# A gated GELU layer on one core: the first slices of x by plain loads in token halves on two queues, all transposed by TensorE

## The chip, the core and the metric

The kernel runs on one NeuronCore of a Trainium2 chip. A core has TensorE (matrix products; PE in the profile, its weight loads PEld), VectorE (DVE), ScalarE (ACT), GpSimd (POOL) and SyncE (SP). SP and ACT also issue the DMAs that bring data from device memory into the core's memory; an issue is shown under SPq or ACTq. The metric is the device time of one execution in microseconds, the median of several runs.

## What is computed

```python
def _gelu(x):
    return jax.nn.gelu(x, approximate=True)

# x: 1 x 2048 x 1024, w_gate and w_up: 1024 x 3584, w_down: 3584 x 1024, all bfloat16
def reference(x, w_gate, w_up, w_down):
    g = jnp.einsum("bsd,df->bsf", x, w_gate)
    u = jnp.einsum("bsd,df->bsf", x, w_up)
    h = _gelu(g) * u
    return jnp.einsum("bsf,fd->bsd", h, w_down)
```

## The kernel before

The 2048 tokens are worked in two halves of 1024, each half in two chunks of 512 (`c`). For one half the kernel first computes h transposed (`hT`: 28 blocks of 128 hidden features by 1024 tokens), then the product with w_down (`down`, line 306) and stores it.

The 28 blocks come in eight groups (`GROUPS`, 3 or 4 blocks). For each block and chunk there are two sums in two PSUM banks, gate and up, of eight matmuls each: over `ko`, the eight slices of 128 of the model dimension (`mm1`, line 103; the stationary operand is a 128x128 piece of weight, the moving one a 128x512 slice of x transposed, `xT[c][ko]`). `Evac` takes a pair of banks through ScalarE and VectorE to hT. Weights go through rings of three (`wg`, `wu`), filled group by group from SP by `wload`; `wd`, the seven 1 MB pieces of w_down, is loaded from SP between the groups of the first half.

x must stand with the model dimension on the partitions. Everywhere but in the opening this is done by DMA transposes from SP (`xload`, line 98). In the opening, chunk 0 of the first half comes in two ways: slices 0 to 5 by plain loads into `xn` (line 186, two slices and all 512 tokens in one DMA of 256 KB) and four 128x128 TensorE transposes each (`turn`, line 230), copied from PSUM to `xT` by VectorE (lines 236, 239, 240; slice 0 in two halves from two banks); slices 6 and 7 by two DMA transposes from SP, after the plain loads. `NTURN` is the number of slices that TensorE turns.

The order of the instructions of each engine is the order in which the program writes them (`manual_schedule`). TensorE begins with six dummy matmuls on a constant (line 174), `turn(0)`, two more dummies of 512 and 256 columns, and then `first_group`: for each slice `ko` the six matmuls of group 0 (three blocks, gate and up), with the turn of slice `ko + 1` set between them. In slice 0 the three gate matmuls go first, then the turn, then the three up matmuls. ScalarE's queue has the load of the activation table (line 180), one small Square on a zeroed tile (`gate`, `gated`, lines 178 and 181), and then its share of the opening's DMAs; SP has the rest. Weights of group 0 are loaded slice by slice (line 192; 96 KB for one slice, 192 KB for two). After the opening's loads SP issues the weights of groups 1 and 2 (line 89), then the eight DMA transposes of chunk 1.

DMAs tell of their landing on eight semaphores in turn, so the ninth issue waits for the first landing, the tenth for the second, and so on.

Group 1 begins with `ahead=2` (gate sums of two blocks, then their up sums) while group 0 is evacuated.

Of the kernel before, what the change touches and what calls it, by code (L numbers as in the profile page):

```python
# [14 lines left out]
def kernel(  # L15
# [11 lines left out]
    nc = tc.nc  # L27
    P = nc.NUM_PARTITIONS
    bf16 = mybir.dt.bfloat16
    f32 = mybir.dt.float32  # L30
    ACT = mybir.ActivationFunctionType
    ALU = mybir.AluOpType

    x2 = x.flatten_outer_dims()
    out2 = out.flatten_outer_dims()
    S, Dm = x2.shape
    Df = w_gate.shape[1]
    NKB = Dm // P
    NFB = Df // P
    SCH = 512  # L40
# [11 lines left out]
    NTMP = 3  # L52
    NST = 4
    WDF = 4
    NWARM = 6
    NTURN = 6
    TPC = SCH // P

    pool = ctx.enter_context(tc.tile_pool(name="sb", bufs=1))
    psum = ctx.enter_context(tc.tile_pool(name="ps", bufs=1, space=bass.MemoryType.PSUM))  # L60

    xT = [[pool.tile([P, SCH], bf16, name=f"xT{c}_{k}") for k in range(NKB)] for c in range(HSC)]
    hT = [pool.tile([P, HS], bf16, name=f"hT{f}") for f in range(NFB)]
    wd = [pool.tile([P, WDF, Dm], bf16, name=f"wd{i}") for i in range(NFB // WDF)]
# [8 lines left out]
    ident = pool.tile([P, P], bf16, name="ident")  # L73
    xn = [pool.tile([P, TPC, 2 * P], bf16, name=f"xn{q}") for q in range(NTURN // 2)]
    banks = [psum.tile([P, 512], f32, name=f"bank{b}") for b in range(8)]
# [3 lines left out]
    def bank():  # L79
        nonlocal nbank  # L80
        b = banks[nbank % 8]
        nbank += 1
        return b
# [12 lines left out]
    def xload(half, c, ko):  # L96
        s0 = half * HS + c * SCH
        nc.sync.dma_start_transpose(
            out=xT[c][ko], in_=x2[s0 : s0 + SCH, ko * P : (ko + 1) * P]
        )  # L100

    def mm1(ps, w, j, c, ko):
        nc.tensor.matmul(  # L103
            ps,
            lhsT=w[:, ko, j * P : (j + 1) * P],
            rhs=xT[c][ko],
            start=(ko == 0),
            stop=(ko == NKB - 1),
        )

# [38 lines left out]
    def pair(wg, wu, j, f, c):  # L149
        g_ps, u_ps = bank(), bank()  # L150
        for ko in range(NKB):
            mm1(g_ps, wg, j, c, ko)
        for ko in range(NKB):
            mm1(u_ps, wu, j, c, ko)
        evac(g_ps, u_ps, f, c)
# [11 lines left out]

    ctx.enter_context(tc.manual_schedule())

    gate = pool.tile([P, SCH], bf16, name="gate")  # L170
    gated = pool.tile([P, 1], f32, name="gated")

    def dummy(b, n=SCH):
        nc.tensor.matmul(b[:, :n], lhsT=warm[:, :P], rhs=warm[:, :n], start=True, stop=True)  # L174

    nc.vector.memset(gate, 0.0)  # L178
    make_identity(nc, ident)
    nc.scalar.preload_act_table(ACT.Sigmoid)  # L180
    nc.scalar.activation(gated, gate[:, :1], ACT.Square)
    for _ in range(NWARM):
        dummy(banks[5])

    def xpart(eng, ko, n):
        eng.dma_start(
            out=xn[ko // 2][:, :, (ko % 2) * P : (ko % 2 + n) * P],
            in_=x2[0:SCH, ko * P : (ko + n) * P].rearrange("(t p) d -> p t d", p=P),
        )

    def wpart(eng, ring, w, ko, n):
        eng.dma_start(
            out=ring[0][:, ko : ko + n, : GROUPS[0] * P],
            in_=w[ko * P : (ko + n) * P, : GROUPS[0] * P].rearrange("(ko ki) f -> ki ko f", ki=P),
        )


    S, A = nc.sync, nc.scalar
    G, U = (wg_ring, w_gate), (wu_ring, w_up)
    xpart(S, 0, 2)  # L200
    wpart(A, *G, 0, 1)
    wpart(S, *U, 0, 1)
    wpart(A, *G, 1, 1)
    wpart(A, *U, 1, 1)
    xpart(S, 2, 2)
    xpart(A, 4, 2)
    wpart(S, *G, 2, 1)
    wpart(S, *U, 2, 1)
    wpart(S, *G, 3, 1)
    wpart(A, *U, 3, 1)  # L210
    wpart(S, *G, 4, 2)
    wpart(A, *U, 4, 2)
    wpart(S, *G, 6, 2)
    wpart(A, *U, 6, 2)
    for ko in range(NTURN, NKB):
        xload(0, 0, ko)
    for n in (1, 2):
        wload(nc.sync, wg_ring, w_gate, n, n)
        wload(nc.sync, wu_ring, w_up, n, n)
# [3 lines left out]
    def turn(ko):  # L223


        tp = [banks[6 + ko % 2].bitcast(bf16)] * 2
        if ko == 0:
            tp = [banks[6].bitcast(bf16), banks[7].bitcast(bf16)]
        for t in range(TPC):
            nc.tensor.transpose(  # L230
                tp[t // (TPC // 2)][:, t * P : (t + 1) * P],
                xn[ko // 2][:, t, (ko % 2) * P : (ko % 2 + 1) * P],
                ident,
            )
        if ko:
            nc.vector.tensor_copy(out=xT[0][ko], in_=tp[0][:, :SCH])  # L236
        else:
            h = SCH // 2
            nc.vector.tensor_copy(out=xT[0][ko][:, :h], in_=tp[0][:, :h])  # L239
            nc.vector.tensor_copy(out=xT[0][ko][:, h:], in_=tp[1][:, h:SCH])  # L240
# [4 lines left out]
    def prefetch(n):  # L245
        if n < len(order):
            wload(nc.sync, wg_ring, w_gate, order[n][1], n)
            wload(nc.sync, wu_ring, w_up, order[n][1], n)

    def first_group():  # L250
        wg, wu = wg_ring[0], wu_ring[0]
        ps = [(bank(), bank()) for _ in range(GROUPS[0])]
        turn(0)
        dummy(banks[5])
        dummy(banks[5], SCH // 2)
        n0 = GROUPS[0]
        for ko in range(NKB):
            steps = [(b, j) for j in range(n0) for b in range(2)]
            if ko == 0:
                steps = [(b, j) for b in range(2) for j in range(n0)]  # L260
            for i, (b, j) in enumerate(steps):
                mm1(ps[j][b], (wg, wu)[b], j, 0, ko)
                if i == (2 if ko == 0 else 1) and ko + 1 < NTURN:
                    turn(ko + 1)
        e = [Evac(ps[j][0], ps[j][1], j, 0) for j in range(GROUPS[0])]
        e[0].square()
        e[1].square()
        e[0].cubic()
        e[0].sigmoid()
        e[1].cubic()  # L270
        e[2].square()
        e[0].gelu()
        e[0].product()
        e[1].sigmoid()
        e[2].cubic()
        e[1].gelu()
        e[1].product()
        e[2].sigmoid()
        e[2].gelu()
        e[2].product()  # L280

    def group(n, chunks, ahead=0):
        g = order[n][1]
        wg, wu = wg_ring[n % NW], wu_ring[n % NW]
        if ahead:
            pairs(wg, wu, range(ahead), STARTS[g], chunks[0])
        for j in range(ahead, GROUPS[g]):
            for c in chunks:
                pair(wg, wu, j, STARTS[g] + j, c)
# [13 lines left out]
    def down(half, ss, c0, cw, k):  # L303
        ps = bank()
        for f in range(NFB):
            nc.tensor.matmul(  # L306
                ps[:, :cw],
                lhsT=hT[f][:, ss * P : (ss + 1) * P],
                rhs=wd[f // WDF][:, f % WDF, c0 : c0 + cw],
                start=(f == 0),  # L310
                stop=(f == NFB - 1),
            )
        store(ps, half * HS + ss * P, c0, cw, k)

    for half in range(NHALF):
        base = half * NG
        if half == 0:
            first_group()
            group(1, [0], ahead=2)
            group(2, [0])  # L320
            for g in range(NG):
                group(g, [1] if g < NW else range(HSC))
                i = g - 1
                if 0 <= i < len(wd):
                    for q in range(i, len(wd) if g == NG - 1 else i + 1):
                        nc.sync.dma_start(
                            out=wd[q],
                            in_=w_down[q * WDF * P : (q + 1) * WDF * P, :].rearrange(
                                "(fo fi) d -> fi fo d", fi=P
                            ),  # L330
                        )
                prefetch(g + 3)
        else:
            for g in range(NG):
                group(base + g, range(HSC))
                prefetch(base + g + 3)
        k = 0
        xnext = [(c, ko) for c in range(HSC) for ko in range(NKB)] if half + 1 < NHALF else []
        for ss in range(HS // P):
            for dc in range(NDC):  # L340
                last = half == NHALF - 1 and ss == HS // P - 1 and dc == NDC - 1
                if last:
                    down(half, ss, dc * DMW, DMW // 2, 1)
                    down(half, ss, dc * DMW + DMW // 2, P, 1)
                    down(half, ss, dc * DMW + DMW - P, P, 0)
                else:
                    down(half, ss, dc * DMW, DMW, k)
                k += 1
                if xnext:
                    c, ko = xnext.pop(0)  # L350
                    xload(half + 1, c, ko)
# [30 lines left out]
```

## Time and profile before

| what | value |
| --- | --- |
| median of three runs | 591.14 us (590.63 to 591.17) |
| the profiled execution | 591.7 us, of which the span from its first instruction to its last 589.9 us |
| matmuls of gate and up in the trace (L103) | 1756, 426.4 us busy |
| matmuls of the down product (L306) | 935, 193.0 us busy |
| TensorE transposes (L230) | 24, 2.7 us busy |
| copies of turned slices, 128x512 (L236) | 5 of 425 ns |
| dummies (L174) | 8, 3.6 us busy |
| DMA transposes (L98) | 26 in all, of these 2 for chunk 0 |
| DMA traffic | 45.51 MB, mean 77 GB/s |

An execution is recorded instruction by instruction. Matmuls overlap in the pipeline, so a matmul's own duration (380 ns for 512 columns) is longer than the distance to the next, and the distance is what counts. A group's row names the line, engine, operation and tiles, the shape, the number, the busy time and mean, and the idle time ahead of it with what ended it. The chain of waits is followed back from the last instruction to what released each one; a stretch on the chain is time that nothing hid. A few matmul records are missing. Idle time of an engine that is off the chain costs nothing by itself.

### The profile page before, as it was taken

The page shows a single profiled execution, that of the slowest core. Times are in us where ns is not written, and L with a number is a line of the kernel's source. Part 1 is how long each engine was busy: PE and PEld are TensorE (multiplying, and loading weights), DVE is VectorE, ACT ScalarE, POOL GpSimd, SP SyncE. Part 2 cuts the span into 40 slices and gives each one's busy share as a digit, 9 for nine tenths or more (in the row PEclk, how much of TensorE's full clock was granted, in tenths as well). Part 3 has the DMA queues.
Part 4 walks back from the last instruction along what each step waited for, and adds up shares of the span by engine and source line. Part 5 has one row for each costly group of instructions (what it writes and reads, how often), then busy time and mean ns, then how long its engine had stood idle before and what let it go on. Part 6 is the DMA issues. An engine that isn't in the chain of part 4 may idle for free.

```text
span 589.9 us, 6587 instructions
## 1 busy us (share of the span) xinstructions
PE 583.4 (99%) x2723; PEld 269.0 (46%) x2776; DVE 244.2 (41%) x361; ACT 147.7 (25%) x243; POOL 0.7 (0%) x6
## 2 busy tenths in 40 slices
PE   9999999999999999999999999999999999999998
PEld 4444444444444444444444444444444444444445
DVE  1765665565656400000046565656556562000000
ACT  1433333333333200000023333333333331000000
POOL 0000000000000000000000000000000000000000
PEclk9999999999999999999999999999999999999999
DMA  8906936055050311111203034214000000000000
GB/s 233 222 10 186 316 104 214 13 202 178 1 178 1 107 48 42 45 46 36 54 19 108 17 126 143 86 57 131 12 1 1 1 2 9 19 27 19 27 19 27
DMA packets 57789, 45.51 MB, mean 77 GB/s; under 512 B 15776, under 2 KB 54176, under 8 KB 57760
## 3 DMA queue, kind: packets, MB, share of 16 engines
q1 hardware_dynamic: 56112, 44.05, 24.8%
q10 hardware_dynamic: 1648, 1.05, 0.6%
q8 instruction: 21, 0.34, 0.2%
q14 instruction: 8, 0.07, 0.0%
HBM read 37.49 MB, written 4.19 MB: 71 GB/s over the span
## 4 chain that ended last, share of the span: by engine, by line
PE 98%; DMA 1%; issue 0%; ACT 0%
PE bank L103 65%; PE bank L306 33%; DMA xn<-in_x_dram 1%; PE bank L230 0%; PE bank L174 0%; ACT st L298 0%
## 5 line engine op out<-in xcount | busy, mean ns | idle before, releaser
L103 PE MATMUL bank<-xT,wg 128*128 128x512 bf16 x880 | 213.8, 380 | 0.9
L103 PE MATMUL bank<-xT,wu 128*128 128x512 bf16 x876 | 212.6, 379 | 1.0
L306 PE MATMUL bank<-wd,hT 128*128 128x512 bf16 (+2 forms) x935 | 193.0, 366 | 0.9
L306 PEld LDWEIGHTS <-hT 128*128 128x128 bf16 x952 | 90.9, 98 | 102.9
L103 PEld LDWEIGHTS <-wg 128*128 128x128 bf16 x896 | 87.8, 98 | 105.6 <-issue 0.6
L103 PEld LDWEIGHTS <-wu 128*128 128x128 bf16 x896 | 87.7, 98 | 105.0
L125 ACT ACTIVATE sq<-bank 128x512 f32<-128x512 f32 x112 | 66.7, 596 | 172.7 <-PE bank L103 166.8
L136 DVE TENSOR_TENSOR tt<-sg,bank 128x512 bf16<-128x512 bf16 x112 | 77.0, 687 | 75.9 <-ACT sg L133 75.8
L128 DVE SCALAR_TENSOR_TENSOR wq<-sq,bank 128x512 f32<-128x512 f32 x112 | 76.9, 687 | 65.2 <-ACT sq L125 65.2
L133 ACT ACTIVATE sg<-wq 128x512 bf16<-128x512 f32 x112 | 70.5, 629 | 88.3 <-DVE wq L128 88.3
L300 DVE CAST st<-bank 128x512 bf16<-128x512 f32 (+2 forms) x17 | 11.1, 652 | 178.3 <-PE bank L306 166.9
L139 DVE TENSOR_TENSOR hT<-tt,bank 128x512 bf16<-128x512 bf16 x112 | 77.0, 687 | 12.4 <-DVE tt L136 0.9
L298 ACT CAST st<-bank 128x512 bf16<-128x512 f32 (+1 forms) x17 | 9.6, 566 | 178.1 <-PE bank L306 178.1
L236 DVE COPY xT<-bank 128x512 bf16<-128x512 bf16 x5 | 2.1, 425 | 6.2 <-PE bank L230 6.2
L174 PE MATMUL bank<-const-bfloat16-1.0 128*128 128x512 bf16 (+1 forms) x8 | 3.6, 601 | 0.8 <-PEq L366 0.8
L230 PEld LDWEIGHTS <-xn 128*128 128x128 bf16 x24 | 2.1, 111 | 2.7 <-DMA xn<-in_x_dram 1.2
L230 PE MATMUL bank<-ident,xn 128*128 128x128 bf16 x24 | 2.7, 247 | 0.3 <-DMA xn<-in_x_dram 0.3
L174 PEld LDWEIGHTS <-const-bfloat16-1.0 128*128 128x128 bf16 x8 | 1.0, 138 | 1.8 <-issue 1.8
L239 DVE COPY xT<-bank 128x256 bf16<-128x256 bf16 x1 | 0.3, 292 | 3.1 <-PE bank L230 3.1
L180 ACT ACT_TABLE_LOAD x1 | 1.3, 1283 | 0.7 <-PEq L366 0.7
L178 DVE MEMSET gate<- 128x256 uint32 x1 | 0.3, 272 | 0.9 <-PEq L366 0.9
masks.py:199 POOL TENSOR_SCALAR_AFFINE_SELECT ident<-ident 128x128 bf16<-128x128 bf16 x1 | 0.3, 292 | 0.1
(7 smaller groups left out, 1.1 us busy)
## 6 DMA issues: line engine op xcount, KB each, us to landing
wg<-in_w_gate_dram SPq DMA_DIRECT2D x8, 1024.0 KB, 5.4
wu<-in_w_up_dram SPq DMA_DIRECT2D x8, 1024.0 KB, 7.0
wd<-in_w_down_dram SPq DMA_DIRECT2D x7, 1024.0 KB, 8.8
wg<-in_w_gate_dram SPq DMA_DIRECT2D x7, 768.0 KB, 4.7
wu<-in_w_up_dram SPq DMA_DIRECT2D x7, 768.0 KB, 6.6
out_dram<-st SPq DMA_DIRECT2D x31, 128.0 KB, 1.7
xn<-in_x_dram SPq DMA_DIRECT2D x2, 256.0 KB, 4.0
xT<-in_x_dram SPq DMA_TRANSPOSE x26, 2.6
```

The source lines that it names most:

```text
L103: nc.tensor.matmul(ps, lhsT=w[:, ko, j * P : (j + 1) * P], rhs=xT[c][ko], start=(ko == 0), stop=(ko == NKB - 1),)
L125: nc.scalar.activation(self.sq, self.g, ACT.Square, scale=GELU_SQRT_C)
L128: nc.vector.scalar_tensor_tensor(out=self.wq, in0=self.sq, scalar=1.0, in1=self.g, op0=ALU.add, op1=ALU.mult)
L133: nc.scalar.activation(self.sg, self.wq, ACT.Sigmoid, scale=GELU_K)
L136: nc.vector.tensor_tensor(out=self.tt, in0=self.sg, in1=self.g, op=ALU.mult)
L139: nc.vector.tensor_tensor(out=self.dst, in0=self.tt, in1=self.u, op=ALU.mult)
L174: nc.tensor.matmul(b[:, :n], lhsT=warm[:, :P], rhs=warm[:, :n], start=True, stop=True)
L230: nc.tensor.transpose(tp[t // (TPC // 2)][:, t * P : (t + 1) * P], xn[ko // 2][:, t, (ko % 2) * P : (ko % 2 + 1) * P], ident,)
L236: nc.vector.tensor_copy(out=xT[0][ko], in_=tp[0][:, :SCH])
L298: nc.scalar.copy(out=st[:, :cw], in_=ps[:, :cw])
L300: nc.vector.tensor_copy(out=st[:, :cw], in_=ps[:, :cw])
L306: nc.tensor.matmul(ps[:, :cw], lhsT=hT[f][:, ss * P : (ss + 1) * P], rhs=wd[f // WDF][:, f % WDF, c0 : c0 + cw], start=(f == 0), stop=(f = ...
```

## The change

The two DMA transposes of chunk 0 go; all eight slices are loaded plainly and turned by TensorE (`NTURN` 8, `xn` one pair larger). Each pair of slices is loaded in two DMAs of 128 KB, tokens 0 to 255 from SP and tokens 256 to 511 from ACT. The order on the two queues is the same: a half of a pair of x, the weights of the two slices that use it (gate from SP, up from ACT), the next pair, and so on; the last two slices of weight come in one DMA each, as before.

The table load moves behind ACT's DMAs, and the zeroed tile with its memset and small Square is dropped. The number of dummies ahead of `turn(0)` stays six (`NWARM` 7, less one); the two after it become 256 and 128 columns in place of 512 and 256.

In slice 0 the three gate matmuls are split into six of 256 columns, first those of tokens 0 to 255 for the three blocks, then those of tokens 256 to 511; `turn(1)` still follows the last of them, ahead of the up matmuls. Only the first of a bank's matmuls carries the start flag.

The first three of the seven wd loads are issued in two halves of 512 KB each.

```diff
--- before.py
+++ after.py
@@ -52,8 +52,11 @@
     NTMP = 3
     NST = 4
     WDF = 4
-    NWARM = 6
-    NTURN = 6
+    NWARM = 7
+    NTURN = 8
+
+
+    NSPLIT = 3
     TPC = SCH // P
 
     pool = ctx.enter_context(tc.tile_pool(name="sb", bufs=1))
@@ -99,12 +102,13 @@
             out=xT[c][ko], in_=x2[s0 : s0 + SCH, ko * P : (ko + 1) * P]
         )
 
-    def mm1(ps, w, j, c, ko):
+    def mm1(ps, w, j, c, ko, t0=0, t1=SCH):
+
         nc.tensor.matmul(
-            ps,
+            ps[:, t0:t1],
             lhsT=w[:, ko, j * P : (j + 1) * P],
-            rhs=xT[c][ko],
-            start=(ko == 0),
+            rhs=xT[c][ko][:, t0:t1],
+            start=(ko == 0 and t0 == 0),
             stop=(ko == NKB - 1),
         )
 
@@ -167,25 +171,17 @@
 
     ctx.enter_context(tc.manual_schedule())
 
-    gate = pool.tile([P, SCH], bf16, name="gate")
-    gated = pool.tile([P, 1], f32, name="gated")
-
     def dummy(b, n=SCH):
         nc.tensor.matmul(b[:, :n], lhsT=warm[:, :P], rhs=warm[:, :n], start=True, stop=True)
 
-
-
-    nc.vector.memset(gate, 0.0)
     make_identity(nc, ident)
-    nc.scalar.preload_act_table(ACT.Sigmoid)
-    nc.scalar.activation(gated, gate[:, :1], ACT.Square)
-    for _ in range(NWARM):
+    for _ in range(NWARM - 1):
         dummy(banks[5])
 
-    def xpart(eng, ko, n):
+    def xpart(eng, ko, n, t0=0, t1=TPC):
         eng.dma_start(
-            out=xn[ko // 2][:, :, (ko % 2) * P : (ko % 2 + n) * P],
-            in_=x2[0:SCH, ko * P : (ko + n) * P].rearrange("(t p) d -> p t d", p=P),
+            out=xn[ko // 2][:, t0:t1, (ko % 2) * P : (ko % 2 + n) * P],
+            in_=x2[t0 * P : t1 * P, ko * P : (ko + n) * P].rearrange("(t p) d -> p t d", p=P),
         )
 
     def wpart(eng, ring, w, ko, n):
@@ -195,25 +191,31 @@
         )
 
 
+
+
     S, A = nc.sync, nc.scalar
     G, U = (wg_ring, w_gate), (wu_ring, w_up)
-    xpart(S, 0, 2)
-    wpart(A, *G, 0, 1)
-    wpart(S, *U, 0, 1)
-    wpart(A, *G, 1, 1)
-    wpart(A, *U, 1, 1)
-    xpart(S, 2, 2)
-    xpart(A, 4, 2)
-    wpart(S, *G, 2, 1)
-    wpart(S, *U, 2, 1)
-    wpart(S, *G, 3, 1)
-    wpart(A, *U, 3, 1)
-    wpart(S, *G, 4, 2)
-    wpart(A, *U, 4, 2)
+
+    def xhalves(ko, n):
+        xpart(S, ko, n, 0, TPC // 2)
+        xpart(A, ko, n, TPC // 2, TPC)
+
+    xhalves(0, 2)
+    for ko in (0, 1):
+        wpart(S, *G, ko, 1)
+        wpart(A, *U, ko, 1)
+    xhalves(2, 2)
+    for ko in (2, 3):
+        wpart(S, *G, ko, 1)
+        wpart(A, *U, ko, 1)
+    xhalves(4, 2)
+    for ko in (4, 5):
+        wpart(S, *G, ko, 1)
+        wpart(A, *U, ko, 1)
+    xhalves(6, 2)
     wpart(S, *G, 6, 2)
     wpart(A, *U, 6, 2)
-    for ko in range(NTURN, NKB):
-        xload(0, 0, ko)
+    nc.scalar.preload_act_table(ACT.Sigmoid)
     for n in (1, 2):
         wload(nc.sync, wg_ring, w_gate, n, n)
         wload(nc.sync, wu_ring, w_up, n, n)
@@ -251,16 +253,19 @@
         wg, wu = wg_ring[0], wu_ring[0]
         ps = [(bank(), bank()) for _ in range(GROUPS[0])]
         turn(0)
-        dummy(banks[5])
         dummy(banks[5], SCH // 2)
+        dummy(banks[5], P)
         n0 = GROUPS[0]
         for ko in range(NKB):
-            steps = [(b, j) for j in range(n0) for b in range(2)]
+            steps = [(b, j, 0, SCH) for j in range(n0) for b in range(2)]
             if ko == 0:
-                steps = [(b, j) for b in range(2) for j in range(n0)]
-            for i, (b, j) in enumerate(steps):
-                mm1(ps[j][b], (wg, wu)[b], j, 0, ko)
-                if i == (2 if ko == 0 else 1) and ko + 1 < NTURN:
+
+                h = SCH // 2
+                steps = [(0, j, t, t + h) for t in (0, h) for j in range(n0)]
+                steps += [(1, j, 0, SCH) for j in range(n0)]
+            for i, (b, j, t0, t1) in enumerate(steps):
+                mm1(ps[j][b], (wg, wu)[b], j, 0, ko, t0, t1)
+                if i == (2 * n0 - 1 if ko == 0 else 1) and ko + 1 < NTURN:
                     turn(ko + 1)
         e = [Evac(ps[j][0], ps[j][1], j, 0) for j in range(GROUPS[0])]
         e[0].square()
@@ -323,12 +328,13 @@
                 i = g - 1
                 if 0 <= i < len(wd):
                     for q in range(i, len(wd) if g == NG - 1 else i + 1):
-                        nc.sync.dma_start(
-                            out=wd[q],
-                            in_=w_down[q * WDF * P : (q + 1) * WDF * P, :].rearrange(
-                                "(fo fi) d -> fi fo d", fi=P
-                            ),
-                        )
+                        n = WDF // 2 if q < NSPLIT else WDF
+                        for f in range(0, WDF, n):
+                            r = (q * WDF + f) * P
+                            nc.sync.dma_start(
+                                out=wd[q][:, f : f + n, :],
+                                in_=w_down[r : r + n * P, :].rearrange("(fo fi) d -> fi fo d", fi=P),
+                            )
                 prefetch(g + 3)
         else:
             for g in range(NG):
```

## The prediction

> **What bounds the kernel now.** I read the page from the top: the span, the busy row of the engines, then the chain that ended last.
>
> ```profile
> span 589.9 us, 6587 instructions
> PE 583.4 (99%) x2723; PEld 269.0 (46%) x2776; DVE 244.2 (41%) x361; ACT 147.7 (25%) x243; POOL 0.7 (0%) x6
> ...
> PE 98%; DMA 1%; issue 0%; ACT 0%
> ```
>
> TensorE is the chain for 98% of the span, so only what TensorE does, or waits for, can move the time. Next comes the chain in order of time (start us, duration us, what). Its first pieces:
>
> ```profile
> 0.74 3.03 DMA xn<-in_x_dram
> 3.81 0.61 PE bank L230 x4
> 4.42 0.64 PE bank L174 x2
> 5.06 1.28 PE bank L103 x3
> 6.34 0.38 PE bank L230 x4
> 6.72 1.11 PE bank L103 x5
> 7.83 0.22 PE bank L230 x4
> 8.05 1.29 PE bank L103 x6
> 9.35 0.22 PE bank L230 x4
> 9.57 1.29 PE bank L103 x6
> ...
> 12.61 8.85 PE bank L103 x41
> ...
> 32.30 10.74 PE bank L103 x49
> 43.04 0.05 issue
> 43.09 10.74 PE bank L103 x49
> ```
>
> After 12.61 us matmuls follow one another without a hole to the end (10.79 us for 49 recorded and, by the spacing, one lost record: 0.216 us each). The change can win or lose in the opening alone. There the reader sees three things. The first slice of x takes 3.03 us to come. The three matmuls from 5.06 take 0.427 us each, those from 8.05 on 0.215: TensorE runs at half speed at first, although the page's clock row reads 9 from the start. And one turn of a slice (four transposes) costs 0.22 us of chain at full speed.
>
> The timeline gives the edge and the hand-over in detail (its starts lie some 0.2 us ahead of the chain's, which counts ends; I use the timeline's from here on):
>
> ```profile
> 0.73 1.28 ACT L180 ACT_TABLE_LOAD   x1 [0.73 <-PEq L366]
> 0.77 2.72 PE L174 MATMUL bank<-const-bfloat16-1.0 128*128 128x512 bf16 x6 [0.77 <-PEq L366]
> 1.17 0.90 ACTq L192 DMA_DIRECT2D wg<-in_w_gate_dram  x2
> 3.81 0.61 PE L230 MATMUL bank<-ident,xn 128*128 128x128 bf16 x4 [0.32 <-DMA xn<-in_x_dram]
> 4.25 0.29 DVE L239 COPY xT<-bank 128x256 bf16<-128x256 bf16 x1 [3.12 <-PE bank L230]
> 4.86 1.48 PE L103 MATMUL bank<-xT,wg 128*128 128x512 bf16 x3
> 6.56 0.81 PE L103 MATMUL bank<-xT,wu 128*128 128x512 bf16 x3
> ```
>
> The first real matmul starts at 4.86. The three from 6.56 need 0.81 in all with their tail, so full speed begins at about 6.5.
>
> **The change, part by part.**
>
> *Landing of the first slices.* Today SP issues all of xn[0] (256 KB) at 0.74 and it lands at 3.77 (0.74 + 3.03). ACT issues nothing before 1.17, because the table load sits ahead of its queue. Changed, both queues issue one half at about 0.74. Later bound: nothing is won, transposes start at 3.81. Earlier bound: the six dummies stream until 0.77 + 6 x 0.427 = 3.33, and no transpose passes them. The windows of a quarter microsecond show 68 to 215 GB/s from 1.75 to 2.75 us and 328 to 363 GB/s after: there is unused rate that a second queue could fill, but nothing shows that it does. I take the middle, 3.57.
>
> By the Trainium skill (DMA: Bandwidth & Descriptors, Rules for kernel authors) loads spread over several issuing engines gain no bandwidth and only issue time, since all run on the same DMA engines; by that rule the slice lands at 3.77 still, and the sum below would be +0.31 in place of +0.17.
>
> *From the transposes to the first matmul.* Today 1.05 us (3.81 to 4.86): four transposes 0.41 and dummies of 512 + 256 columns, 0.64. The dummies shrink to 256 + 128 columns, 0.32 at the same rate, so TensorE is free after 0.73. The first half's copy ends at 4.25 + 0.29 = 4.54, 0.73 after the first transpose; the new half-width matmul needs only this half. With 0.04 for the hand-over I take 0.77: 3.57 + 0.77 = 4.34. It also needs gate slice 0. That is ACT's first issue today and lands 2.9 us after 1.17 (the shortest in the tile's row), 4.07; changed, it is SP's second, behind half of x, where the up slice stands today (1.25 + 3.1 = 4.35). So the first matmul starts at 4.36, with bounds 4.10 (early landing) and 4.58 (late landing): 0.50 us earlier than today, bounds 0.76 and 0.28.
>
> *What half a microsecond is worth.* Until 6.5 TensorE does half the work per time. The stretch after: six half-width matmuls, 1.28 as the three full ones (a 256-column dummy took 0.22, twice that is one full), to 5.64; turn 1 at 0.43 to 6.07; one up matmul at 0.43 to 6.50; two at 0.216 to 6.93. Today the second slice begins at 7.24. The gain is 0.31; taking off the 0.03 by which today's spacing exceeds the sum leaves 0.28 (bounds 0.14 and 0.53; the upper one if the clock steps before the work starts, so that all counts). Turn 1's copy runs 0.20 after its transposes for 0.42 us, to 6.69, before 6.93.
>
> *Two more turns.* Slices 6 and 7 become eight more transposes on TensorE. A slice with a turn lasts 9.35 - 7.83 = 1.52 us on the chain, six matmuls alone 6 x 0.216 = 1.30: a turn costs 0.22, two of them +0.45 with rounding. Their two copies (0.42 each) fall on a VectorE that idles about 1.1 us between such copies, and the turn runs a slice ahead: no cost. Without that cover each would cost at most 0.42.
>
> *Costs of nothing.* The two DMA transposes leave SP's queue (7.70 to 10.19 us); no matmul waited for them, so no gain. What stood behind them, the weights of groups 1 and 2 and chunk 1's transposes, moves up by at most 2.5 us, and group 1 begins at 16.98 waiting for nothing. The table load (1.28) moves behind ACT's eleven issues; the last issue stands near 9 us if the queue keeps today's pace (its last is at 6.54, with eight issues), so it ends about 10.5, and the first Square comes at 16.31: almost 6 us of cover. The gate memset and the early Square go from engines that idle. Three of the wd loads are split: three more issues of some 0.6 us on SP, which waits for matmuls 238 us in total.
>
> *New waits.* Eight transfers are in flight at first: SP issues five up to 3.23, ACT three up to 2.55, and ACT's next comes at 3.79, just after the first landed. Changed, the first eight are x, gate 0, up 0, gate 1, up 1 and the second pair of x, all in halves or pairs; gate 2 is issued when the first half of x lands. Behind a waiting issue stand only later slices' loads. The tightest is the second pair of x, for turn 2 at 6.93 + 0.43 = 7.36: today it lands 5.0 us after its issue at 1.79, at 6.79; changed, it is issued near 2.25 with fewer bytes ahead, so between 6.0 and 7.25. Gate 2 (needed 8.5), x 4 (10.4), x 6 (13.4) have over a microsecond each.
>
> *Sum:* -0.28 + 0.45 = **+0.17 us** on the profiled execution (bounds -0.08 and +0.31). That execution took 591.7 us, 1.8 more than its span, and lies 0.56 above the median of 591.14. Runs below it may well be those whose clock steps earlier, where the earlier start counts in full (-0.50 + 0.45 = -0.05). Between +0.17 and -0.05 I put +0.06 on the median: **591.2 us**.
>
> **The rivals.**
>
> *The halves land no earlier* (3.77). The rate rows after 2.75 us, already at 330 to 360, speak for it; the slow first microsecond speaks against. +0.31: 591.4.
>
> *The full clock comes earlier.* TensorE stops at 3.33 and waits until 3.81 today; with the hole closed the step could come sooner. Floor: first matmul at 4.10, all of it at full rate: 48 x 0.216 + 7 x 0.22 = 11.9, group 1 from 16.0 where it starts at 17.19 today, counting the matmul: -1.2 on 591.7, or 590.5. Against it: nothing in the trace says that the hole delayed the step.
>
> *The full clock comes later: slower.* The place is the stretch up to 6.5. There are now 384 fewer dummy columns, and transposes fill a greater part. If the step waits once more as long as it took from the end of the hole (6.56 - 3.81 = 2.75 us), each microsecond costs half: +1.38, with +0.17 it is +1.55, 592.7. It decides from a delay of 2.0 us on. Against it: TensorE is at least as busy as today.
>
> The Trainium skill (TensorE: Matmul & The Clock Gate, Part 1) says that the clock is gated to half until a free-running window of about 3.4 us has been busy; one window later would be an estimated 1.7 us more, one earlier as much less, by that page. The trace agrees on the factor (0.427 against 0.216) and cannot show the window.
>
> *The second pair of x comes late.* Turn 2 then waits, and all behind it. At 5.0 us after 2.25 it is just in time; each further microsecond costs one. With 0.5 late: 591.7. The fewer bytes ahead speak against it.
>
> **How the numbers follow.** What can be told from no change here is 0.2%, 1.2 us: below 589.96 is faster, above 592.32 slower. Forecast 0.56 (its own range 590.8 to 591.7), halves no earlier 0.10, clock earlier 0.16, clock later 0.12, x late 0.06. Half of "earlier" may pass its floor by scatter (three runs spread over 0.54 us, and the profiled one lies 0.5 above them): faster 0.08. Later 0.12 and a third of "x late" make slower 0.14. Same 0.78. For 8 in 10 the range goes from 590.3, under the floor, to 592.4, short of the later clock.
>
> **What would show it.** Right: six 128x256 gate matmuls starting between 4.10 and 4.58; 32 transposes, a turn at 0.22 in the chain for slices 6 and 7; no DMA wait after 4.4; group 1 within 0.4 us of 17.19. Wrong: a DMA piece in the chain after the first matmul; matmuls spaced at 0.43 beyond 7 us; a wait of the first gate matmul for weights over 0.2 us; any hole after group 1 starts.

## The result and the profile after

The changed kernel takes 592.09 us (median of 15 runs, 591.53 to 593.01) against 591.14 us (15 runs, 590.63 to 591.73): ratio 1.0017, 95% interval 1.0010 to 1.0024, or +0.95 us with an interval of about 0.6 to 1.4. That is inside the predicted range and inside the 0.2% that the prediction counted as no change, but some sixteen times the +0.06 us that it forecast, and it is a loss that the interval separates from zero.

The head of the changed kernel's page, and under it the chain that ended last, followed back from 25 us (start us, duration us, what):

```profile
span 590.3 us, 6616 instructions
...
PE 583.2 (99%) x2733; PEld 269.0 (46%) x2787; DVE 244.9 (41%) x362; ACT 147.9 (25%) x242; POOL 0.7 (0%) x6
...
PE 96%; DMA 3%; issue 1%; ACTq 0%; ACT 0%
```

```profile
0.73 0.49 ACTq L182
...
1.25 0.52 ACTq L188
...
1.80 0.45 ACTq L188
...
2.28 4.83 DMA xn<-in_x_dram
7.11 0.02 issue
7.13 3.39 DMA wu<-in_w_up_dram
10.53 0.02 issue
10.54 7.03 DMA wg<-in_w_gate_dram
17.57 0.05 issue
17.62 2.33 PE bank L107 x10
```

This is the reading that matters. Before, the opening's chain was one load of x and then TensorE without a break. Now it has no TensorE in it at all until 17.62 us: it goes through issues and landings. The ACT half of x's second pair is issued at 2.28 as the eighth transfer and lands at 7.11; the up weights of slice 4 wait for that landing, are issued at 7.13 and land at 10.53; the gate weights of group 1 (line 92) wait for that, are issued at 10.54 and land at 17.57; only then can group 1 begin. Each step is the same mechanism: eight transfers in flight, the next issue waits for an older landing.

TensorE's side, from the timeline of the changed kernel:

```profile
3.62 0.54 PE L232 MATMUL bank<-ident,xn 128*128 128x128 bf16 x4
...
4.29 0.82 PE L107 MATMUL bank<-xT,wg 128*128 128x256 bf16 x6
...
6.16 0.39 PE L107 MATMUL bank<-xT,wg 128*128 128x512 bf16 x1 [0.18 <-DMA wg<-in_w_gate_dram]
...
6.93 0.51 PE L232 MATMUL bank<-ident,xn 128*128 128x128 bf16 x4 [0.17 <-DMA xn<-in_x_dram]
...
16.82 0.38 PE L107 MATMUL bank<-xT,wu 128*128 128x512 bf16 x1
17.62 3.63 PE L107 MATMUL bank<-xT,wg 128*128 128x512 bf16 x15 [0.42 <-DMA wg<-in_w_gate_dram]
```

The first gate matmul starts at 4.29 where it started at 4.86. Then TensorE waits three times: for gate slice 1 until 6.16 and for the second pair of x until 6.93 (each comes 0.34 us after TensorE could have gone on), and for group 1's weights: from 16.82 to 17.62 are 0.80 us, of which a matmul uses 0.22, so the hole is 0.58. The bracket shows 0.42, because a matmul's recorded duration reaches past the point where the next could start.

The same places in the timeline of the kernel before, the last matmuls of group 0, the first of group 1 and the issue of its gate weights on SP:

```profile
10.23 0.58 SPq L89 DMA_DIRECT2D wg<-in_w_gate_dram  x1
...
16.98 0.38 PE L103 MATMUL bank<-xT,wu 128*128 128x512 bf16 x1
17.19 1.03 PE L103 MATMUL bank<-xT,wg 128*128 128x512 bf16 x4
```

From group 1 on nothing differs: both executions need 572.7 us from its first matmul to the end of the span (589.9 - 17.19 and 590.3 - 17.62).

The two profiled executions are not alike in one respect. The six half-width gate matmuls from 4.29 take 0.82 us with their tail, so TensorE runs at full rate there; in the execution shown of before it did so only from about 6.5. Group 1 begins 0.43 us later although TensorE had some two microseconds more at full rate. The medians, not this pair of spans, give the size of the loss. The profiled execution before is a slow one of its kind: the median of the spans of the kernel before, in the rounds of the experiments, is 589.2 to 589.4 us, that of the changed kernel 590.3. With 572.7 us from group 1 on, these spans put the start of group 1 at an estimated 16.5 to 16.7 us before and 17.6 after, and that is the whole +0.95.

### The profile page after: what moved, and what is told of

It is laid out like the page before. It is cut to its first block, busy times and chain, and to the rows that moved or that the text cites. A ratio compares the mean times of both kernels' runs of the same rounds, so it can differ in the third digit from the quotient of the medians.

```text
span 590.3 us, 6616 instructions
## 1 busy us (share of the span) xinstructions
PE 583.2 (99%) x2733; PEld 269.0 (46%) x2787; DVE 244.9 (41%) x362; ACT 147.9 (25%) x242; POOL 0.7 (0%) x6
## 4 chain that ended last, share of the span: by engine, by line
PE 96%; DMA 3%; issue 1%; ACTq 0%; ACT 0%
PE bank L107 63%; PE bank L311 33%; DMA wg<-in_w_gate_dram 1%; DMA xn<-in_x_dram 1%; DMA wu<-in_w_up_dram 1%; ACTq L188 0%; ACTq L182 0%; ACT st L303 0%
## 5 line engine op out<-in xcount | busy, mean ns | idle before, releaser
L107 PE MATMUL bank<-xT,wg 128*128 128x512 bf16 (+1 forms) x880 | 212.6, 378 | 1.5 <-DMA wg<-in_w_gate_dram 0.6
L175 PE MATMUL bank<-const-bfloat16-1.0 128*128 128x512 bf16 (+2 forms) x8 | 3.0, 529 | 0.8 <-PEq L372 0.8
```

Of the source, the lines that this page charges most:

```text
L107: nc.tensor.matmul(ps[:, t0:t1], lhsT=w[:, ko, j * P : (j + 1) * P], rhs=xT[c][ko][:, t0:t1], start=(ko == 0 and t0 == 0), stop=(ko == NKB ...
```

## The experiments

Each was timed in five rounds beside the kernel before; "against before" is the difference of the medians on the same chip, with the ratio's interval. Most have eleven runs, `two_extra` four.

**The late weights.** Group 1's gate weights in two transfers:

```diff
-    for n in (1, 2):
-        wload(nc.sync, wg_ring, w_gate, n, n)
-        wload(nc.sync, wu_ring, w_up, n, n)
...
+    for ko in (0, NKB // 2):
+        nc.sync.dma_start(
+            out=wg_ring[1][:, ko : ko + NKB // 2, :cw],
...
+    wload(nc.sync, wu_ring, w_up, 1, 1)
+    wload(nc.sync, wg_ring, w_gate, 2, 2)
+    wload(nc.sync, wu_ring, w_up, 2, 2)
```

> The changed kernel with the gate weights of group 1 loaded in two DMAs of four slices each (384 KB) in place of one of 768 KB; nothing else differs. Theory A (group 1 waits for its gate weights, which land as one at 17.57 us): its first matmul can start when the first four slices are there; group 1 starts near 17.05 instead of 17.62, the time falls by about 0.5 us, to +0.45 us against the kernel before. Theory B (the loss is the two more turns, 0.45 us of TensorE, and the rest is scatter): group 1's start moves with nothing here, the time stays at +0.95 us.

Measured: 591.46 us, +0.47 against before (ratio 1.0007, 0.9998 to 1.0016). The hole ahead of group 1 is gone, in the timeline of this run:

```profile
16.33 0.38 PE L107 MATMUL bank<-xT,wu 128*128 128x512 bf16 x1
16.54 2.25 PE L107 MATMUL bank<-xT,wg 128*128 128x512 bf16 x9
```

0.21 us from one to the other is a matmul's spacing. A smaller wait is left inside group 1: nine matmuls 0.216 us apart end after 2.11 us and took 2.25, for the second transfer, issued at 10.53, took 7.0 us to land. About half of the loss was this one wait, as theory A said. Theory B's +0.95 lies on the edge of the interval, and B falls by the trace, since the hole that it gave no part of the loss is gone; on the same chip the changed kernel with its wd loads undivided, told of below, took 592.05 us, 0.59 more.

**A later start of TensorE.** If the wait for these weights ends the opening, a slower start should cost next to nothing:

```diff
-        dummy(banks[5], SCH // 2)
-        dummy(banks[5], P)
+        dummy(banks[5])
+        dummy(banks[5], SCH // 2)
...
-                steps = [(0, j, t, t + h) for t in (0, h) for j in range(n0)]
-                steps += [(1, j, 0, SCH) for j in range(n0)]
+                steps = [(b, j, 0, SCH) for b in range(2) for j in range(n0)]
...
```

> The changed kernel with TensorE's start of before: dummies of 512 and 256 columns, three whole gate matmuls in slice 0; loads as changed. Theory A and D (the changed opening ends when group 1's gate weights land): the first gate matmul comes 0.3 us later and group 1 starts where it did, +0.95 to +1.1 us against the kernel before. Rival (TensorE's own work sets the changed opening): +1.25 us.

Measured: 592.29 us, +1.10 against before (1.0018, 1.0010 to 1.0027), at the upper edge of what A and D expect; the interval does not shut out the rival's 1.25. The profile decides it:

```profile
16.03 0.38 PE L107 MATMUL bank<-xT,wu 128*128 128x512 bf16 x1
17.40 0.82 PE L107 MATMUL bank<-xT,wg 128*128 128x512 bf16 x3 [0.99 <-DMA wg<-in_w_gate_dram]
```

This execution does not show a late start: x landed sooner, the transposes began at 3.29 where they began at 3.62, and the first gate matmul came at 4.30 as in the changed kernel. It shows the other side of the same question. TensorE was done with group 0 at 16.03 + 0.22, 0.8 us sooner than in the changed kernel's profile, and it waited 1.15 us for the same load. Group 1 starts with the landing (17.4 here, 17.6 there) and not with TensorE. A part of the +1.10 lies outside the recorded span: the median of the spans is 590.0 us, 0.6 above the kernel before and no more than the changed kernel's 590.3, where the rival would have them longer.

**The turns.** First the transposes of slices 6 and 7 put back:

```diff
-    NTURN = 8
+    NTURN = 6
...
-    xhalves(6, 2)
...
+    for ko in range(NTURN, NKB):
+        xload(0, 0, ko)
```

> The changed kernel with slices 6 and 7 again by DMA transposes after the last plain loads (six turns on TensorE), everything else as changed: halves, order, split wd. Theory B (turns): 0.45 us less TensorE, so +0.5 us against the kernel before. Theory A (gate weights of group 1): the two transposes hold SP's queue for about 2.5 us ahead of that load, which then lands no earlier than 17.6; group 1 starts at 17.6 or later and the time stays at +0.95 us or more.

Measured: 590.96 us, -0.03 (1.0000, 0.9991 to 1.0008). Both theories are off. B counted 0.45 of the 0.95; A had the load land no earlier than 17.6. SP's timeline in this run:

```profile
8.89 2.49 SPq L101 DMA_TRANSPOSE xT<-in_x_dram  x2
11.43 0.58 SPq L92 DMA_DIRECT2D wg<-in_w_gate_dram  x1
```

and TensorE's:

```profile
16.05 0.38 PE L107 MATMUL bank<-xT,wu 128*128 128x512 bf16 x1
16.46 0.82 PE L107 MATMUL bank<-xT,wg 128*128 128x512 bf16 x3
```

The load is issued 0.9 us later than in the changed kernel, and yet group 1 begins at 16.46, after a hole of 0.2 us: it comes in 5.0 us instead of 7.0. The transposes did hold the queue up, and the load behind them came faster by more. Why it came faster is not shown. That the earlier loads drain while SP is busy with the transposes does not explain it by itself: when the load was issued, six earlier pieces of 832 KB together had yet to land, in this run and in the changed kernel alike.

With both, six turns and the weights in two transfers:

> Slices 6 and 7 again by DMA transposes, and group 1's gate weights in two DMAs of four slices; else as changed. Theory A (turns and late gate weights add up): the run with the transposes back still had a hole of 0.20 us ahead of group 1; it goes, so -0.2 us against the kernel before. Rival (what that run won came from the turns alone and its hole is covered elsewhere): 0.0 us.

Measured: 590.90 us, -0.29 (0.9997, 0.9988 to 1.0006). No hole ahead of group 1 is left, but the interval does not tell this from before. On another chip it came out on the other side:

> Six turns and group 1's gate weights in two DMAs once more, on the same chip as the run with the added transposes: -0.2 to -0.3 us against the kernel before, and 0.45 us less than with them.

Measured: 591.36 us, +0.31 (1.0003, 0.9994 to 1.0012). The two together stand at zero: this version can't be told from the kernel before.

Then the turns' TensorE work by itself, added to that version. The first build of it had a mistake of mine, a third set of transposes:

```diff
                     turn(ko + 1)
+                elif i == 1 and ko + 1 < NKB:
...
+                    for t in range(TPC):
+                        nc.tensor.transpose(
+                            tp[:, t * P : (t + 1) * P], xn[2][:, t, P : 2 * P], ident
+                        )
```

> The kernel with six turns and group 1's gate weights in two DMAs, with eight transposes of slice 5 added on TensorE, four in slice 5 and four in slice 6, at the place where the turns of slices 6 and 7 would stand; nothing reads them. They are the two turns' TensorE work by itself, with no load and no copy. If TensorE bounds that opening, they cost 2 x 0.22 = 0.45 us against the run without them, +0.15 to +0.25 us against the kernel before. Rival (the opening waits for data there, so they are hidden): no difference.

Measured: 597.78 us, +6.73 (1.0117, 1.0102 to 1.0133). The condition also holds in slice 0, where the added transposes read x's third pair, which had not come:

```profile
4.49 0.62 PE L107 MATMUL bank<-xT,wg 128*128 128x256 bf16 x2
9.35 0.61 PE L282 MATMUL bank<-ident,xn 128*128 128x128 bf16 x4 [4.23 <-DMA xn<-in_x_dram]
...
12.31 0.63 PE L107 MATMUL bank<-xT,wg 128*128 128x512 bf16 x1
12.73 0.63 PE L107 MATMUL bank<-xT,wu 128*128 128x512 bf16 x1
```

It says nothing of the turns' price, but it shows what an early hole costs: more than its own 4.4 us (the matmuls of 256 columns ahead stand 0.21 apart, and 9.35 - 4.70 - 0.21 is 4.44), because at 12.3 us the matmuls still stand 0.42 us apart. TensorE had not yet come to its full rate ahead of the hole, and comes to it the later for it. The mended one has the condition `NTURN <= ko + 1 < NKB`:

> Six turns and group 1's gate weights in two DMAs, with exactly eight transposes of slice 5 added, four in slice 5 and four in slice 6, where the turns of slices 6 and 7 stand in the changed kernel; nothing reads them. (The run before with added transposes had a third set of four in slice 0, which waited for the third pair of x.) The two runs without them came out at -0.3 and +0.3 us against the kernel before. If TensorE bounds the opening, the two turns cost 0.45 us: +0.3 to +0.6 us. Rival (hidden behind data): 0.0 us.

Measured: 591.57 us, +0.47 (1.0009, 1.0000 to 1.0018). Its timeline gives the price directly:

```profile
13.19 0.38 PE L107 MATMUL bank<-xT,wu 128*128 128x512 bf16 x1
13.41 0.39 PE L282 MATMUL bank<-ident,xn 128*128 128x128 bf16 x4
13.63 0.38 PE L107 MATMUL bank<-xT,wg 128*128 128x512 bf16 x1
```

0.44 us from matmul to matmul across a turn instead of 0.22: a turn is 0.22, two are 0.44. The median, with the two runs without the added transposes taken at zero, agrees with the 0.45 of the prediction, but its interval, 0 to 1.1 us, says little; the spacing shows the price.

**The shape of the loads.** The kernel before with slices 6 and 7 loaded plainly, whole, and turned:

```diff
-    NTURN = 6
+    NTURN = 8
...
+    xpart(S, 6, 2)
     wpart(S, *G, 6, 2)
     wpart(A, *U, 6, 2)
-    for ko in range(NTURN, NKB):
-        xload(0, 0, ko)
```

> The kernel before with slices 6 and 7 loaded plainly in one DMA of 256 KB from SP and turned by TensorE; no halves, order, dummies and table load as before. Theory A: 16 issues stand ahead of group 1's gate weights instead of 22 and no transposes, so these are issued earlier than 10.23 us and land before 16.5; TensorE pays two turns, group 1 starts near 17.65 by TensorE alone, +0.45 us. Theory C (the halves on two queues make gate slice 1 and the second pair of x late, and this is the loss): also no hole after the first matmul, +0.45 us. If dropping the transposes is by itself the loss: +0.95 us, with a hole ahead of group 1.

Measured: 591.86 us, +0.87 (1.0016, 1.0007 to 1.0025). Its profile has no wait for data after the first matmul, group 1 at 17.05, so by it the two turns alone, +0.45, would be expected; the interval reaches from 0.4 to 1.5. Half of the 0.87 is the turns. Some 0.2 lies outside the recorded span, whose median is 589.9 us against 589.2, +0.7; what the last quarter of a microsecond is this run does not show.

The changed kernel with the first pair alone in halves, the other loads in the order and sizes of before:

```diff
     xhalves(0, 2)
-    for ko in (0, 1): ...
-    xhalves(2, 2) ...
+    wpart(A, *G, 0, 1)
+    wpart(S, *U, 0, 1)
...
+    xpart(S, 2, 2)
+    xpart(A, 4, 2)
...
+    wpart(S, *G, 4, 2)
+    wpart(A, *U, 4, 2)
+    xpart(S, 6, 2)
```

> The changed kernel, all eight slices turned by TensorE, but only the first pair of x comes in halves; the later pairs come whole (256 KB), and the weights in the order and the sizes of before (slices 4 and 5 in one DMA). Sixteen transfers stand ahead of group 1's gate weights in place of 22. Theory D (with eight in flight, small pieces leave too few bytes on the way, and the rate dips): by 10.0 us about 2200 KB have come instead of 1800, group 1's gate weights land before 16.0, no hole ahead of group 1, +0.4 us against the kernel before. Rival (the weights are late because 256 KB more of x come plainly ahead of them): they land near 17.5 again, +0.95 us.

Measured: 591.97 us, +0.78 (1.0013, 1.0004 to 1.0022). Seventeen transfers stand ahead of group 1's gate weights, one more than the expectation counts. Theory D was right on these weights, with no hole ahead of them, and wrong on the time, because the wait moved to another load, gate slices 4 and 5:

```profile
10.79 0.38 PE L107 MATMUL bank<-xT,wu 128*128 128x512 bf16 x1
11.74 0.39 PE L107 MATMUL bank<-xT,wg 128*128 128x512 bf16 x1 [0.57 <-DMA wg<-in_w_gate_dram]
```

0.95 us apart, a hole of 0.73. What the loads did as a whole stands in the windows from 4 to 16 us of four kernels (busy time of PE, PEld, DVE, ACT, POOL, the clock row, the share of the DMA engines and, last, GB/s), the changed kernel first, then the one before, `coarse` and `before_turn8`:

```profile
4.00:16.00 12.00, 11.60 (x78) 6.22 (x78) 3.47 (x9) 1.28 (x1) 0.00 (x0) 1.00 0.91 255
```

```profile
4.00:16.00 12.00, 11.95 (x68) 6.18 (x68) 2.63 (x7) 0.00 (x0) 0.00 (x0) 1.00 0.98 277
```

```profile
4.00:16.00 12.00, 11.04 (x75) 5.81 (x74) 3.31 (x9) 1.28 (x1) 0.00 (x0) 1.00 0.99 299
```

```profile
4.00:16.00 12.00, 11.95 (x77) 6.30 (x77) 3.48 (x9) 0.00 (x0) 0.00 (x0) 1.00 1.02 306
```

Without DMA transposes, the order in whole pairs moves 299 and 306 GB/s, the order in halves 255 (262 to 275 in the three other runs that have it with eight turns). But the rate does not sort the kernels by how late the weights are: `turn6` moves 248 GB/s and has them at 16.4. Theory D's bytes come out (by the windows up to 10 us, 215 GB/s in `coarse` and 186 in the changed kernel, that is about 2150 and 1860 KB), and yet `late_start` and `wg1_two`, with 218 GB/s up to there, have the whole of group 1's gate weights at 17.4 and 17.5 only. What sorts them is the single load, from its issue to its landing:

| kernel | loads ahead of it | issued, us | to landing, us | landed, us |
| --- | --- | --- | --- | --- |
| changed | 22, all plain | 10.54 | 7.0 | 17.6 |
| `late_start` | 22, all plain | 10.27 | 7.1 | 17.4 |
| `wd_whole` | 22, all plain | 10.62 | 6.7 | 17.3 |
| `coarse` | 17, all plain | 8.92 | 6.9 | 15.8 |
| `before_turn8` | 16, all plain | 8.01 | 7.1 | 15.1 |
| before | 17, the last two DMA transposes | 10.23 | 5.7 | 15.9 |
| `turn6` | 22, the last two DMA transposes | 11.43 | 5.0 | 16.4 |

Without DMA transposes ahead of it the load takes 6.7 to 7.1 us in either order, so the bytes of slices 6 and 7 alone do not make it too late; what the changed order with its 22 smaller transfers adds is a later issue, by about 2 us. With DMA transposes ahead it takes 5.0 to 5.7 us. Whether the number, the size or the order of the pieces delays the issue was not tried apart.

**The early start alone.** The kernel before with the changed start, first with the halves of the first pair:

```diff
-    xpart(S, 0, 2)
+    xhalves(0, 2)
...
-        dummy(banks[5])
         dummy(banks[5], SCH // 2)
+        dummy(banks[5], P)
```

(with the half-width gate matmuls, the table load behind ACT's loads, and without the memset and the small Square)

> The kernel before with the start of the changed one alone: first pair of x in halves on SP and ACT, table load behind ACT's DMAs, dummies of 256 and 128 columns, the first gate matmuls in halves of 256 columns. Order and sizes of all else, the DMA transposes of slices 6 and 7 and wd as before. Theory A and D: TensorE starts 0.5 us earlier and nothing later is late: -0.3 to -0.5 us against the kernel before. Rival (the opening is bound by data from slice 1 on, so an earlier start is given back in a wait): 0.0 us, with a hole before 8 us.

Measured: 591.35 us, +0.16 (1.0004, 0.9996 to 1.0013). A gain of 0.3 us is shut out. TensorE started early and gave it back:

```profile
4.30 0.83 PE L107 MATMUL bank<-xT,wg 128*128 128x256 bf16 x6
...
5.19 0.81 PE L107 MATMUL bank<-xT,wu 128*128 128x512 bf16 x3
6.32 0.39 PE L107 MATMUL bank<-xT,wg 128*128 128x512 bf16 x1 [0.32 <-DMA wg<-in_w_gate_dram]
```

Three up matmuls at full rate end their turn at 5.19 + 0.65 = 5.84; gate slice 1 is there at 6.3. With TensorE's two edits alone and all loads as before:

> The kernel before with two edits of TensorE alone: the two dummies after the first turn of 256 and 128 columns, and slice 0's gate matmuls in halves. All loads as before. The first gate matmul starts 0.28 us earlier (x lands at 3.77 still). If no data is late behind it, -0.14 to -0.28 us; if gate 1 or the second pair of x bounds, 0.0 us.

Measured: 591.19 us, +0.14 (1.0000, 0.9991 to 1.0009). The expected gain of 0.14 to 0.28 is too small for this interval to shut out; the rival's zero lies in its middle, and the profile has waits for up slice 1 and for the second pair of x.

**The divided wd loads.** `NSPLIT = 0`:

> The changed kernel with the first three wd loads undivided as before. All theories: no matmul waits for wd, so no difference, +0.95 us against the kernel before within 0.3 us, and group 1 starts near 17.6.

Measured: 592.05 us, +1.06 (1.0022, 1.0013 to 1.0030), a hole of 0.56 us ahead of group 1 at 17.33: the changed kernel's own time. The divided wd loads do nothing here.

## Why the prediction was right, and where it was not

**Bound.** Right: TensorE from group 1 on, and the loss arose before it.

**First landing and first matmul.** The transposes started at 3.62 (forecast 3.57) and the first gate matmul at 4.29 (4.36, bounds 4.10 to 4.58). That the first lies so near is in part luck. The middle was taken between two bounds without a mechanism, and the start scatters: 3.28 to 3.72 us in the eleven profiles with halves, 3.47 to 3.81 in the three with the whole pair from SP.

**What the half microsecond is worth** (-0.28): nothing could be shown of it. The step worked out when the later data are needed for a TensorE at half rate until 6.5. At full rate from 4.3, as in the profiled execution, gate slice 1 is needed at 5.8 and came so that its matmul started at 6.16; the second pair of x was there from 6.93 with its first half and landed as a whole at 7.11, within the forecast's 6.0 to 7.25, and was needed at 6.6 rather than 7.36. The margins should have been taken for the earliest start and the full rate together. `first_pair` and `short_start` show the early start given back.

**Two more turns** (+0.45): right; the spacing in `turn_price` gives 0.22 each.

**Costs of nothing.** Here is the step that failed. The prediction put that what stood behind the DMA transposes "moves up by at most 2.5 us, and group 1 begins at 16.98 waiting for nothing", and counted no cost. Group 1's gate weights were issued at 10.54 where they were at 10.23, because their issue hangs on a landing two links up a chain of eight in flight, and they took 7.0 us where they had taken 5.7. The prediction named that chain, checked the slices of group 0 along it, and stopped one load short. The hole is 0.58 us and dividing the load took about half of the loss away, 0.5 of 0.95. The other edits of this part did cost nothing: the wd loads by experiment, and the table load ran at 9.99 us, ahead of a first Square at 16.15.

**The sum.** +0.45 for the turns, +0.5 for the late weights and about 0 for the early start make the +0.95 measured. The rival that named a late load had the right mechanism and the wrong load. Neither the halves landing at 3.77 nor a later clock is needed for the loss; the clock came earlier in the profiled execution and gave nothing, since the opening then waited for data. The spans say the same: the start of group 1 moves from an estimated 16.5 to 16.7 us to 17.6.

**Right by the range, not by its mechanism.** The prediction named its own signs. Six half-width gate matmuls from 4.29 and 32 transposes came. The signs of being wrong came too: DMA pieces in the chain after the first matmul, up to 17.57, waits for DMAs after 4.4, and group 1 at 17.62, 0.43 from 17.19 where 0.4 was allowed. That 592.09 lies between 590.3 and 592.4 is luck: the range runs from the floor of an earlier clock to short of a later one, and what filled its upper part, the late weights of group 1, is no term of it.

**Three figures of its working.** The 16.98 is the start of group 0's last matmul; group 1 starts at 17.19, as the prediction has it elsewhere. The upper bound of 0.53 for the earlier start is less than the 0.76 that the earliest start, counted in full, would give. And ACT has seven issues in the kernel before, not eight. None of them decides the result.

## What to carry to other kernels

Where a fixed number of transfers is in flight, follow the chain of issues to the first load behind the part that you change, not only to the last load inside it: here the issue of that load came about 2 us later with the split loads than with the order in whole pairs. Work out when data are needed with TensorE at its fastest. And a start that is made earlier is worth only as much as the next load allows.

## What the runs showed of the hardware

TensorE's full rate does not come at a fixed point after its first instruction. Six dummies start at 0.77 or 0.78 us in the executions told of here, and the first gate matmuls ran at full rate from 4.29 in the changed kernel, at half rate in `turn_price`:

```profile
4.50 1.49 PE L107 MATMUL bank<-xT,wg 128*128 128x256 bf16 x6
```

1.49 us for what took 0.82. Nor is it the changed dummies: `late_start` has the dummies of before and ran at full rate from 4.30. The clock row of the page, where there is one, reads 9 or 1.00 throughout, and the spacing shows the step. The records of the granted clock, which ten of the fourteen kept traces hold, agree with the spacing: the full clock begins at 6.55 us in the kernel before, 6.23 in `turn_price`, 3.65 in the changed kernel, 3.99 in `late_start` and 13.4 after the hole of `two_extra`, and in all ten it lasts 171 or 172 times 3.413 us, to a thousandth of that. So the clock changes on a grid of 3.41 us that does not begin with the kernel. The Trainium skill (TensorE: Matmul & The Clock Gate, Part 1) tells of a window that runs free of the kernel's start, some 3.4 us long; these records agree with that.

The 768 KB of group 1's gate weights took 5.0 to 5.7 us from issue to landing where SP issued two DMA transposes just ahead of them, and 6.7 to 7.1 where it issued none. The cause is open.

That loads issued from SP and ACT side by side bring no more bandwidth is what the Trainium skill says (DMA: Bandwidth & Descriptors, Rules for kernel authors). The first pair of x agrees: whole from SP it landed at 3.4 to 3.8 us in three profiles, and the later of its two halves from SP and ACT at 3.4 to 4.0 us in eleven.
